# Folding and transform of the next sequence in pieces between chunks, with activation and sums placed after the block-end copies

## Chip, cores and metric

One Trainium2 chip, one of its cores. The metric is the device time of one execution of the whole kernel in microseconds, median of three runs.

## What is computed

Eight sequences of 3008 rows by 256 features go through a two-dimensional Fourier transform of which the real part is kept; each row of the result then goes through a two-layer block with a squared relu between the layers.

```python
batch, seq, dim = (8, 3008, 256)          # x
X = np.fft.fft(x, axis=1)
X = np.fft.fft(X, axis=2)
x = X.real.reshape(B * S, D)
h = x @ w_in                              # 256 x 2048
r = np.maximum(h, 0.0)
return (r * r) @ w_out                    # 2048 x 256
```

All in float32. A matmul of float32 appears in the profile as two records (two passes), and two weight loads.

## The kernel before

**Setting up.** The weights w_in are rounded on DVE (`rounded`, lines 137 to 154, nine DVE instructions for a load of 512 KB), and TensorE folds the transform over the features into them (`G1`, `G2`, `gE`). The tables of the transform over the rows stay in SBUF. w_out is rounded in the same way, a piece of it at the head of each of the first eight steps (`load_wout`).

**A sequence in two stages.** First the transform over the rows. `fold` (lines 191 to 212) takes one of the six row tiles of a sequence and adds and subtracts it with itself: eight DVE instructions with both inputs in SBUF, one small ScalarE copy of edge columns (line 204), and, on SP's queue, the load of the row tile that comes four later (`load_x`). It leaves `wP` and `wQ`. Then six groups of `dft_ops` (lines 214 to 259) multiply them with the tables: `even_n` is three matmuls into a PSUM tile `pd` and a ScalarE copy to `da`; `odd_n` is three matmuls into a second `pd` and two DVE instructions that write `Pt`, `Qt` or `Et`, a sequence's transform. The pool of `pd` has two buffers, and the transposes `po` of `store` use the same two.

**Then 48 steps**: six blocks of 251 or 250 columns by eight values of j. A step has these parts:

- `front` (lines 262 to 282): two chunks (the loop over h). Each is two matmuls into a PSUM tile `ph` (two buffers, so one for each chunk) and three DVE instructions (lines 275, 277, 278) that write half of the tile `g`. Then ScalarE applies relu and square to all of `g` in place.
- `combine` (lines 286 to 295): four GpSimd instructions form the sums `s` of `g`, on the left side of a Strassen-like product.
- `back` (lines 299 to 312): seven matmuls of `g` and `s` with w_out, accumulated over the eight j in four PSUM tiles mA to mD. `back` runs two steps behind `front` (LAG = 2).
- At a block's end `gather` (lines 314 to 333): ScalarE copies mA and mB to SBUF (`sA`, `sB`), DVE forms three sums `u`, GpSimd four sums `c`. Two steps later `store` transposes `c` on TensorE into `po`, copies it on ScalarE and sends it out on SP's queue.

**What sets the order.** The scheduling is manual: every engine runs its instructions in the order in which the program issues them. The main loop (lines 359 to 382) issues, for step i: `front(i)`, `combine(i)`, then the work for the next sequence, then `store` if one is due, then `back(i-2)` and, at a block's end, `gather`. The next sequence's folds stand whole behind the fronts of steps 1, 2, 4, 5, 7 and 8 of a sequence; its transform stands in rows of five operations at steps 10 and 18 and three at step 26. The last sequence has no such work, as none comes after it.

Of the kernel before, what the change touches and what calls it, by code (L numbers as in the profile page):

```python
# [42 lines left out]
def kernel(  # L43
# [12 lines left out]
    nc = tc.nc  # L56
    B, NROW, _, D = x.shape
# [5 lines left out]
    H = D // 2  # L63
    NJ = NFC // 2
    CH = 256
    CK = 251
    NT = 6
    NX = 4
# [7 lines left out]
    fp = ctx.enter_context(tc.tile_pool(name="fp", bufs=2))  # L76
    wp = ctx.enter_context(tc.tile_pool(name="wp", bufs=NT))
# [5 lines left out]
    op = ctx.enter_context(tc.tile_pool(name="op", bufs=2))  # L83
# [106 lines left out]

    def fold(b, t):

        rows = TILES[t][1]
        r = slice(0, rows)
        v = xt[b, t]
        s = fp.tile([P, 2, D], F32, name="fs", tag="fs")
        d = fp.tile([P, 2, D], F32, name="fd", tag="fd")
        tt(out=s[r], in0=v[r, 0::2], in1=v[r, 1::2], op=ALU.add)
        tt(out=d[r], in0=v[r, 0::2], in1=v[r, 1::2], op=ALU.subtract)
        if b * NT + t + NX < B * NT:  # L200
            load_x(*divmod(b * NT + t + NX, NT))
        sc = fp.tile([P, 2, H + 1], F32, name="sc", tag="sc")
        dc = fp.tile([P, 2, H - 1], F32, name="dc", tag="dc")
        nc.scalar.copy(sc[r, :, 0:H + 1:H], s[r, :, 0:H + 1:H])
        tt(out=sc[r, :, 1:H], in0=s[r, :, 1:H], in1=s[r, :, D - 1:H:-1], op=ALU.add)
        tt(out=dc[r], in0=d[r, :, 1:H], in1=d[r, :, D - 1:H:-1], op=ALU.subtract)
        wP = wp.tile([P, 2, H + 1], F32, name="wP", tag="wP")
        wQ = wp.tile([P, 2, H - 1], F32, name="wQ", tag="wQ")
        for kp in range(2):
            tt(out=wP[r, kp], in0=sc[r, 0], in1=sc[r, 1], op=ALU.subtract if kp else ALU.add)  # L210
            tt(out=wQ[r, kp], in0=dc[r, 0], in1=dc[r, 1], op=ALU.add if kp else ALU.subtract)  # L211
        folded[b, t] = (wP, wQ)

    def dft_ops(b):

        ops = []

        def start():
            PQE[b] = [pq.tile([n, NKT], F32, name=nm, tag=nm)
                      for nm, n in (("Pt", P), ("Qt", P - 1), ("Et", P))]  # L220

        def group(kp, which, st):
            nk = NK[kp]
            n = P - 1 if which == 1 else P
            tab = sinT if which == 1 else cosT

            def product(half):
                ps = psd.tile([P, 512], F32, name="pd", tag="d")[0:n, 0:nk]
                for i in range(3):
                    t = 3 * half + i  # L230
                    rows = TILES[t][1]
                    w = folded[b, t][which % 2][0:rows, kp]
                    w = w[:, H:H + 1].to_broadcast([rows, n]) if which == 2 else w[:, 0:n]
                    nc.tensor.matmul(ps, w, tab[0:rows, kp, t, 0:nk],  # L234
                                     start=i == 0, stop=i == 2)
                return ps

            def even_n():
                ps = product(0)
                st["a"] = hp.tile([P, NK[0]], F32, name="da", tag="da", bufs=2)[0:n, 0:nk]  # L240
                nc.scalar.copy(st["a"], ps)  # L241
# [12 lines left out]
            return [even_n, odd_n]  # L254

        for kp in range(2):
            for which in range(3):
                ops += group(kp, which, {})
        return [start] + ops


    def front(b, k0, n, j):

        pt, qt, et = PQE[b]
        ks = slice(k0, k0 + n)
        g = gp.tile([P, 2, 2, CK], F32, name="g", tag="g")
        for h in range(2):
            fc = j + NJ * h
            fs = slice(fc * P, (fc + 1) * P)
            ps = psh.tile([P, 2, CH], F32, name="ph", tag="h")  # L270
            hP, hQ = ps[:, 0, 0:n], ps[:, 1, 0:n]
            nc.tensor.matmul(hP, G1[:, fs], pt[:, ks], start=True, stop=True)  # L272
            nc.tensor.matmul(hQ, G2[:, fs], qt[:, ks], start=True, stop=True)  # L273
            t = hp.tile([P, CK], F32, name="he", tag="he")[:, 0:n]
            nc.vector.scalar_tensor_tensor(out=t, in0=et[:, ks], scalar=gE[:, fc:fc + 1], in1=hP,  # L275
                                           op0=ALU.mult, op1=ALU.add)
            tt(out=g[:, h, 0, 0:n], in0=t, in1=hQ, op=ALU.add)  # L277
            tt(out=g[:, h, 1, 0:n][:, ::-1], in0=t, in1=hQ, op=ALU.subtract)  # L278
        v = g[:, :, :, 0:n]
        act(v, v, AF.Relu)  # L280
        act(v, v, AF.Square)  # L281
        return g

    def combine(n, g):
# [4 lines left out]
        gt(out=s1, in0=g21, in1=g22, op=ALU.add)  # L291
# [7 lines left out]
    def back(n, j, g, s):  # L299

        if j == 0:
            for nm in ("mA", "mB", "mC", "mD"):
                acc[nm] = psm.tile([P, 2, CH], F32, name=nm, tag=nm)
        for nm, i, w, v in (("mA", 0, wout[:, 0, j, 0:H], g[:, 0, 0]),
                            ("mA", 1, wout[:, 1, j, 0:H], g[:, 1, 0]),
                            ("mB", 0, wsum[:, 2, j], g[:, 1, 1]),
                            ("mB", 1, wout[:, 0, j, H:D], s[:, 0]),
                            ("mC", 0, wsum[:, 0, j], s[:, 1]),
                            ("mC", 1, wsum[:, 1, j], s[:, 2]),
                            ("mD", 0, wout[:, 1, j, H:D], s[:, 3])):  # L310
            nc.tensor.matmul(acc[nm][:, i, 0:n], w, v[:, 0:n], start=j == 0 and i == 0, stop=j == NJ - 1,  # L311
                             skip_group_check=True)
# [38 lines left out]
    for f in [lambda t=t: fold(0, t) for t in range(NT)] + dft_ops(0):  # L351
# [6 lines left out]
    dft = []  # L358
    for i in range(len(steps) + LAG + 3):
        at = i % per  # L360
        if i < len(steps):
            b, k0, n, j = steps[i]
            if i < NJ:
                load_wout(i)
            g = front(b, k0, n, j)
            flight.append((b, k0, n, j, g, combine(n, g)))
            if b + 1 < B:
                if at < 9 and at % 3:
                    fold(b + 1, at // 3 * 2 + at % 3 - 1)
                if at == 10:  # L370
                    dft = dft_ops(b + 1)
        if at >= 10 and at % NJ == 2:
            for f in dft[:5]:
                f()
            dft = dft[5:]
        while finished and finished[0][0] <= i:
            store(*finished.pop(0)[1:])
        if i >= LAG and flight:
            b, k0, n, j, g, s = flight.pop(0)
            back(n, j, g, s)  # L380
            if j == NJ - 1:
                finished.append((i + 2, b, k0, n, gather(n)))


# [61 lines left out]
```

## Time and profile before

| | |
|---|---|
| median of three runs | 2365.93 us (2365.11 to 2368.36) |
| the profiled execution: its own time | 2366.93 us |
| the profiled execution: span of its instructions | 2365.2 us |
| mean granted TensorE clock | 0.959 |
| PE, busy (9504 matmul records) | 2138.7 us, 90% |
| DVE, busy | 1310.8 us, 55% |
| POOL, busy | 1168.7 us, 49% |
| ACT, busy | 920.7 us, 39% |

PE is the matmul side of TensorE and PEld its weight loads; DVE is VectorE, ACT ScalarE, POOL GpSimd, SP the queue of transfers. A row of the profile's groups or of the timeline names line, engine, operation and tiles (out<-in); a bracket gives the idle time of the engine ahead of it, and who ended it. A window's row gives the busy time of each engine with its number of instructions, and PEclk, the share of TensorE's full clock that was granted.

### The profile page before, as it was taken

Reading aid. Unit: us, or ns where it says so; the run is one execution under the profiler, and the core shown is the slowest. Engines: PE = TensorE matmul, PEld = TensorE weight load, DVE = VectorE, ACT = ScalarE, POOL = GpSimd, SP = SyncE. Lnnn points to the kernel's source line nnn. Section 1 sums busy time; section 2 is a strip of 40 time slices with the busy share of each in tenths; the row PEclk is TensorE's granted clock in tenths of the full one; section 3 lists DMA queues with packets and bytes.
Section 4 is the critical chain, followed back from the end, with each engine's and each line's share of the span. In section 5 each row is a group of like instructions: output and inputs, shape, how many; then the busy total and the mean of one; then the engine's idle time right before and its main releaser. Section 6 shows DMA issues by size and latency. Waiting matters only on the chain.

```text
span 2365.2 us, 26858 instructions
## 1 busy us (share of the span) xinstructions
PE 2138.7 (90%) x9504; PEld 1788.6 (76%) x9504; DVE 1310.8 (55%) x3076; ACT 920.7 (39%) x1065; POOL 1168.7 (49%) x1776
## 2 busy tenths in 40 slices
PE   3656999989998899979999799988999889999998
PEld 2334788767887788867888688876888777888887
DVE  5587445664457545584456744566445844455553
ACT  0012344433443344434344334443344333444453
POOL 0044356544565445544456445654456545556655
PEclk7778999999999999999999899999999999999999
DMA  5211000110001000020000100011000000000000
GB/s 189 70 62 44 9 18 10 42 37 10 10 18 44 27 9 18 10 61 9 10 18 27 44 10 18 10 44 36 9 10 18 27 10 9 18 10 18 10 18 18
DMA packets 38371, 64.31 MB, mean 27 GB/s; under 512 B 3285, under 2 KB 27605, under 8 KB 37725
## 3 DMA queue, kind: packets, MB, share of 16 engines
q1 hardware_dynamic: 35981, 54.63, 7.7%
q0 software_dynamic: 1440, 7.72, 0.9%
q8 instruction: 74, 1.21, 0.2%
q14 instruction: 60, 0.49, 0.1%
q10 hardware_dynamic: 816, 0.26, 0.0%
HBM read 37.96 MB, written 24.64 MB: 26 GB/s over the span
## 4 chain that ended last, share of the span: by engine, by line
PE 71%; DVE 17%; ACT 7%; POOL 2%; issue 1%; DMA 1%; ACTq 0%; DVEq 0%; SPq 0%; POOLq 0%
PE ph L272 12%; PE ph L273 11%; PE mA L311 11%; PE mB L311 11%; PE mC L311 11%; PE mD L311 6%; PE pd L234 5%; ACT g L280 3%; ACT g L281 3%; DVE g L277 2%; DVE he L275 2%; DVE g L278 2%; PE po L345 2%; DVE wP L210 2%; DVE wQ L211 1%
## 5 line engine op out<-in xcount | busy, mean ns | idle before, releaser
L280 ACT ACTIVATE g<-g 128x1004 f32<-128x1004 f32 (+1 forms) x384 | 399.2, 1040 | 1246.2 <-DVE g L278 845.7
L291 POOL TENSOR_TENSOR s<-g 128x251 f32<-128x251 f32 (+1 forms) x384 | 243.0, 633 | 1001.1 <-ACT g L281 913.7
L275 DVE SCALAR_TENSOR_TENSOR he<-Et,gE,ph 128x251 f32<-128x251 f32 (+1 forms) x768 | 362.5, 472 | 656.3 <-PE ph L273 656.0
L272 PE MATMUL ph<-Pt,G 128*128 128x251 f32 (+1 forms) x1536 | 472.5, 389 | 106.2 <-DVE g L278 104.9
L273 PE MATMUL ph<-Qt,G 127*128 127x251 f32 (+1 forms) x1536 | 466.1, 385 | 0.0
L272 PEld LDWEIGHTS ph<-Pt,G 128*128 128x128 f32 x1536 | 291.0, 194 | 170.5 <-DVE g L278 136.0
L311 PE MATMUL mC<-s,wsum 128*128 128x251 f32 (+1 forms) x1536 | 392.7, 377 | 14.8 <-DVE u L326 14.8
L281 ACT ACTIVATE g<-g 128x1004 f32<-128x1004 f32 (+1 forms) x384 | 399.1, 1039 | 12.1
L311 PE MATMUL mA<-g,wout 128*128 128x251 f32 (+1 forms) x1536 | 393.5, 378 | 0.0
L277 DVE TENSOR_TENSOR g<-he,ph 128x251 f32<-128x251 f32 (+1 forms) x768 | 320.5, 417 | 57.3 <-POOL s L293 0.5
L311 PEld LDWEIGHTS mC<-s,wsum 128*128 128x128 f32 x1536 | 292.4, 191 | 52.6 <-issue 17.0
L273 PEld LDWEIGHTS ph<-Qt,G 127*128 127x128 f32 x1536 | 300.7, 196 | 39.4
L311 PEld LDWEIGHTS mA<-g,wout 128*128 128x128 f32 x1536 | 288.6, 192 | 44.0 <-ACT sA L321 4.1
L278 DVE TENSOR_TENSOR g<-he,ph 128x251 f32<-128x251 f32 (+1 forms) x768 | 314.1, 409 | 0.0
L292 POOL TENSOR_TENSOR s<-s,g 128x251 f32<-128x251 f32 (+1 forms) x384 | 281.0, 732 | 30.1
L293 POOL TENSOR_TENSOR s<-g 128x251 f32<-128x251 f32 (+1 forms) x384 | 287.9, 750 | 0.0
L294 POOL TENSOR_TENSOR s<-g,s 128x251 f32<-128x251 f32 (+1 forms) x384 | 247.1, 644 | 0.0
L311 PE MATMUL mD<-s,wout 128*128 128x251 f32 (+1 forms) x768 | 226.4, 376 | 0.0
L311 PE MATMUL mB<-g,wsum 128*128 128x251 f32 (+1 forms) x768 | 226.0, 375 | 0.0
L311 PE MATMUL mB<-s,wout 128*128 128x251 f32 (+1 forms) x768 | 224.6, 374 | 0.0
L234 PE MATMUL pd<-cosT,wP 128*128 128x377 f32 (+5 forms) x384 | 140.9, 513 | 27.0 <-ACT da L241 15.1
L311 PEld LDWEIGHTS mB<-g,wsum 128*128 128x128 f32 x768 | 146.6, 191 | 18.2
(63 smaller groups left out, 1382.0 us busy)
## 6 DMA issues: line engine op xcount, KB each, us to landing
xt<-in_x_dram SPq DMA_DIRECT2D x28, 512.0 KB
out_dram<-os SPq DMA_DIRECT2D x96, 125.0 KB
out_dram<-os SPq DMA_DIRECT2D x80, 126.0 KB
raw<-in_moe_w_in_dram SPq DMA_DIRECT2D x8, 512.0 KB
raw<-in_moe_w_out_dram SPq DMA_DIRECT2D x8, 512.0 KB
xt<-in_x_dram SPq DMA_DIRECT2D x7, 484.0 KB
xt<-in_x_dram SPq DMA_DIRECT2D x7, 480.0 KB
cosT<-in_cos_s_dram POOLq DMA_DIRECT2D x2, 1131.0 KB, 18.0
```

What stands on the lines that cost most here:

```text
L234: nc.tensor.matmul(ps, w, tab[0:rows, kp, t, 0:nk], start=i == 0, stop=i == 2)
L272: nc.tensor.matmul(hP, G1[:, fs], pt[:, ks], start=True, stop=True)
L273: nc.tensor.matmul(hQ, G2[:, fs], qt[:, ks], start=True, stop=True)
L275: nc.vector.scalar_tensor_tensor(out=t, in0=et[:, ks], scalar=gE[:, fc:fc + 1], in1=hP, op0=ALU.mult, op1=ALU.add)
L277: tt(out=g[:, h, 0, 0:n], in0=t, in1=hQ, op=ALU.add)
L278: tt(out=g[:, h, 1, 0:n][:, ::-1], in0=t, in1=hQ, op=ALU.subtract)
L280: act(v, v, AF.Relu)
L281: act(v, v, AF.Square)
L292: gt(out=s2, in0=s1, in1=g11, op=ALU.subtract)
L293: gt(out=s3, in0=g11, in1=g21, op=ALU.subtract)
L294: gt(out=s4, in0=g12, in1=s2, op=ALU.subtract)
L311: nc.tensor.matmul(acc[nm][:, i, 0:n], w, v[:, 0:n], start=j == 0 and i == 0, stop=j == NJ - 1, skip_group_check=True)
```

## The change

`fold` no longer issues anything by itself: it returns six pieces, each with a nominal cost, and `dft_ops` returns its operations with such costs. `front` calls `between()` after each of its two chunks; `between` issues pieces from the list of the next sequence as the costs fall due, at an even pace over the sequence's 96 chunks less six (in the first sequence over 80 less six, since nothing is issued in its first eight steps). The edge copy goes from ScalarE to DVE. Relu and square move from `front` to `combine`, and `combine(i)` is issued at the end of step i: after the store, `back(i-2)` and the block-end copies and sums.

```diff
     def fold(b, t):
...
-        tt(out=s[r], in0=v[r, 0::2], in1=v[r, 1::2], op=ALU.add)
-        tt(out=d[r], in0=v[r, 0::2], in1=v[r, 1::2], op=ALU.subtract)
-        if b * NT + t + NX < B * NT:
-            load_x(*divmod(b * NT + t + NX, NT))
...
-        nc.scalar.copy(sc[r, :, 0:H + 1:H], s[r, :, 0:H + 1:H])
...
+        def f_s():
+            v = xt[b, t]
+            tt(out=new(fp, "fs", [P, 2, D])[r], in0=v[r, 0::2], in1=v[r, 1::2], op=ALU.add)
+
+        def f_d():
+            v = xt[b, t]
+            tt(out=new(fp, "fd", [P, 2, D])[r], in0=v[r, 0::2], in1=v[r, 1::2], op=ALU.subtract)
+            if b * NT + t + NX < B * NT:
+                load_x(*divmod(b * NT + t + NX, NT))
+
+        def f_sc():
+            s, sc = st["fs"], new(fp, "sc", [P, 2, H + 1])
+            nc.vector.tensor_copy(sc[r, :, 0:H + 1:H], s[r, :, 0:H + 1:H])
...
+        return [(0.7, f_s), (0.7, f_d), (0.5, f_sc), (0.4, f_dc), (0.6, f_p), (0.6, f_q)]
...
-            return [even_n, odd_n]
+            return [(0.6, even_n), (1.2, odd_n)]
...
-    def front(b, k0, n, j):
+    def front(b, k0, n, j, between):
...
             tt(out=g[:, h, 1, 0:n][:, ::-1], in0=t, in1=hQ, op=ALU.subtract)
+            between()
+        return g
...
+    def combine(n, g):
         v = g[:, :, :, 0:n]
         act(v, v, AF.Relu)
         act(v, v, AF.Square)
-        return g
...
+    def ahead(b):
+        return [piece for t in range(NT) for piece in fold(b, t)] + dft_ops(b)
...
+    side, spent, pace = [], 0.0, 0.0
+
+    def between():
+
+        nonlocal spent
+        if i < NJ:
+            return
+        spent -= pace
+        while side and spent <= 0:
+            t, f = side.pop(0)
+            f()
+            spent += t
...
     for i in range(len(steps) + LAG + 3):
-        at = i % per
         if i < len(steps):
             b, k0, n, j = steps[i]
             if i < NJ:
                 load_wout(i)
-            g = front(b, k0, n, j)
-            flight.append((b, k0, n, j, g, combine(n, g)))
-            if b + 1 < B:
-                if at < 9 and at % 3:
-                    fold(b + 1, at // 3 * 2 + at % 3 - 1)
-                if at == 10:
-                    dft = dft_ops(b + 1)
-        if at >= 10 and at % NJ == 2:
-            for f in dft[:5]:
-                f()
-            dft = dft[5:]
+            if i % per == 0:
+                assert not side
+                side = ahead(b + 1) if b + 1 < B else []
+                spent, pace = 0.0, sum(t for t, _ in side) / (2 * (per - (0 if i else NJ)) - 6)
+            g = front(b, k0, n, j, between)
         while finished and finished[0][0] <= i:
             store(*finished.pop(0)[1:])
         if i >= LAG and flight:
...
+            at, g_, s_ = flight.pop(0)
+            back(at[2], at[3], g_, s_)
+            if at[3] == NJ - 1:
+                finished.append((i + 2, *at[:3], gather(at[2])))
+        if i < len(steps):
+            flight.append(((b, k0, n, j), g, combine(n, g)))
```

On DVE, in step 2 of the second sequence before the change, a whole fold stands between two fronts (`he` and `g` are a chunk's three instructions, `fs` to `wQ` the fold's tiles):

```order
L278 TENSOR_TENSOR g<-he,ph 128x251
L198 TENSOR_TENSOR fs<-xt 128x512
L199 TENSOR_TENSOR fd<-xt 128x512
L205 TENSOR_TENSOR sc<-fs 128x2x127
L206 TENSOR_TENSOR dc<-fd 128x254
L210 TENSOR_TENSOR wP<-sc 128x129
L211 TENSOR_TENSOR wQ<-dc 128x127
L210 TENSOR_TENSOR wP<-sc 128x129
L211 TENSOR_TENSOR wQ<-dc 128x127
L275 SCALAR_TENSOR_TENSOR he<-Et,gE,ph 128x251
```

On DVE after the change, in steps 3 and 4 of the second sequence, there is one piece of that fold between two chunks (the same three instructions for a chunk, now lines 295, 297 and 298):

```order
L298 TENSOR_TENSOR g<-he,ph 128x251
L224 TENSOR_TENSOR wP<-sc 128x129 x2
L295 SCALAR_TENSOR_TENSOR he<-Et,gE,ph 128x251
L297 TENSOR_TENSOR g<-he,ph 128x251
L298 TENSOR_TENSOR g<-he,ph 128x251
L295 SCALAR_TENSOR_TENSOR he<-Et,gE,ph 128x251
L297 TENSOR_TENSOR g<-he,ph 128x251
L298 TENSOR_TENSOR g<-he,ph 128x251
L229 TENSOR_TENSOR wQ<-dc 128x127 x2
L295 SCALAR_TENSOR_TENSOR he<-Et,gE,ph 128x251
```

The eight fold instructions in a row have become pieces of one or two, with three or six of the front's instructions between them.

On PE before the change, at step 10 of a sequence, the products of two groups of the transform stand in one row behind the front (`ph`) and ahead of the back (`mA` and so on):

```order
L272 MATMUL ph<-Pt,G_104 128x251
L273 MATMUL ph<-Qt,G_105 128x251
L234 MATMUL pd<-cosT,wP 128x377 x6
L234 MATMUL pd<-sinT,wQ 127x377 x6
L311 MATMUL mA<-g,wout 128x251 x2
```

On PE after the change, at step 35 of the second sequence, one product of three matmuls stands behind the front, here with a store's transposes (`po`) right behind it:

```order
L293 MATMUL ph<-Qt,G_105 128x251
L254 MATMUL pd<-cosT,wP 128x377 x3
L366 MATMUL po<-ident,c 126x128 x8
L332 MATMUL mA<-g,wout 128x251 x2
L332 MATMUL mB<-g,wsum 128x251
```

Twelve products that stood in three rows are spread over steps 29 to 43, one to a step at most, and this one has come to stand ahead of a store.

On ACT before the change, at a block's end, the copies `sA` and `sB` stand behind the relu and square of the step in which they are issued, and the copies `da` of the transform follow two at a time:

```order
L280 ACTIVATE g<-g 128x1004
L281 ACTIVATE g<-g 128x1004
L321 COPY sA<-mA 128x502
L322 COPY sB<-mB 128x502
L280 ACTIVATE g<-g 128x1004
L281 ACTIVATE g<-g 128x1004
L241 COPY da<-pd 128x377
L241 COPY da<-pd 127x377
```

On ACT after the change, at the same block's end (lines 306 and 307 are relu and square):

```order
L307 ACTIVATE g<-g 128x1004
L342 COPY sA<-mA 128x502
L343 COPY sB<-mB 128x502
L306 ACTIVATE g<-g 128x1004
L307 ACTIVATE g<-g 128x1004
L306 ACTIVATE g<-g 128x1004
```

The two copies now come ahead of that step's relu and square, and no `da` copy follows them here.

More of the change, by code (lines that the diff above doesn't have):

```diff
@@ L194, in fold @@
         r = slice(0, rows)
[L195 to L198, printed above, removed]
-        tt(out=d[r], in0=v[r, 0::2], in1=v[r, 1::2], op=ALU.subtract)
-        if b * NT + t + NX < B * NT:
-            load_x(*divmod(b * NT + t + NX, NT))
-        sc = fp.tile([P, 2, H + 1], F32, name="sc", tag="sc")
-        dc = fp.tile([P, 2, H - 1], F32, name="dc", tag="dc")
@@ L204, in fold @@
-        nc.scalar.copy(sc[r, :, 0:H + 1:H], s[r, :, 0:H + 1:H])
[L205 to L211, printed above, removed]
@@ L212, in fold, with new @@
-        folded[b, t] = (wP, wQ)
+        st = {}
+        def new(pool, nm, shape):
+            st[nm] = pool.tile(shape, F32, name=nm, tag=nm)
+            return st[nm]
+        def f_s():
[6 more added lines that the diff above has]
+                load_x(*divmod(b * NT + t + NX, NT))
@@ new lines, in f_sc, with f_dc, f_p @@
+        def f_sc():
+            s, sc = st["fs"], new(fp, "sc", [P, 2, H + 1])
+            nc.vector.tensor_copy(sc[r, :, 0:H + 1:H], s[r, :, 0:H + 1:H])
+            tt(out=sc[r, :, 1:H], in0=s[r, :, 1:H], in1=s[r, :, D - 1:H:-1], op=ALU.add)
+        def f_dc():
+            d = st["fd"]
+            tt(out=new(fp, "dc", [P, 2, H - 1])[r], in0=d[r, :, 1:H], in1=d[r, :, D - 1:H:-1], op=ALU.subtract)
+        def f_p():
+            sc, wP = st["sc"], new(wp, "wP", [P, 2, H + 1])
+            for kp in range(2):
+                tt(out=wP[r, kp], in0=sc[r, 0], in1=sc[r, 1], op=ALU.subtract if kp else ALU.add)
@@ L214, in dft_ops, with f_q @@
+        def f_q():
+            dc, wQ = st["dc"], new(wp, "wQ", [P, 2, H - 1])
+            for kp in range(2):
+                tt(out=wQ[r, kp], in0=dc[r, 0], in1=dc[r, 1], op=ALU.add if kp else ALU.subtract)
+            folded[b, t] = (st["wP"], wQ)
+        return [(0.7, f_s), (0.7, f_d), (0.5, f_sc), (0.4, f_dc), (0.6, f_p), (0.6, f_q)]
     def dft_ops(b):
@@ L258, in dft_ops @@
                 ops += group(kp, which, {})
-        return [start] + ops
-    def front(b, k0, n, j):
+        return [(0.0, start)] + ops
+    def front(b, k0, n, j, between):
         pt, qt, et = PQE[b]
@@ L281, in front @@
         act(v, v, AF.Square)
-        return g
-    def combine(n, g):
         s = sp.tile([P, 4, CK], F32, name="s", tag="s")
@@ L349, in store @@
                 nc.sync.dma_start(out=out[row + c0:row + c1], in_=os_[c0 - o:c1 - o, i])
-    for f in [lambda t=t: fold(0, t) for t in range(NT)] + dft_ops(0):
+    def ahead(b):
+        return [piece for t in range(NT) for piece in fold(b, t)] + dft_ops(b)
+    for _, f in ahead(0):
         f()
@@ L356 @@
     per = len(BLOCKS) * NJ
+    side, spent, pace = [], 0.0, 0.0
[8 more added lines that the diff above has]
+            spent += t
     flight, finished = [], []
-    dft = []
     for i in range(len(steps) + LAG + 3):
-        at = i % per
         if i < len(steps):
@@ L378 @@
         if i >= LAG and flight:
[L379 to L382, printed above, removed]
+            at, g_, s_ = flight.pop(0)
[4 more added lines that the diff above has]
+            flight.append(((b, k0, n, j), g, combine(n, g)))
 _INS = ['x', 'moe_w_in', 'moe_w_out', 'cos_s', 'sin_s', 'cos_d', 'sin_d', 'alt_d']
```

## Prediction

> **What bounds the kernel now.** I read the page first, then the windows by stage, the waits of PE, and the timeline where PE stood still.
>
> ```profile
> PE 2138.7 (90%) x9504; PEld 1788.6 (76%) x9504; DVE 1310.8 (55%) x3076; ACT 920.7 (39%) x1065; POOL 1168.7 (49%) x1776
> 0.00:115.05 115.05, 59.23 (x167) 31.97 (x168) 61.41 (x134) 9.89 (x21) 6.19 (x16) 0.76 0.39 133
> 115.05:206.10 91.05, 45.43 (x150) 35.43 (x148) 81.45 (x152) 14.93 (x18) 35.79 (x59) 0.76 0.18 58
> 206.10:436.85 230.75, 221.36 (x991) 186.24 (x992) 115.45 (x286) 96.12 (x109) 118.34 (x182) 0.98 0.06 16
> 436.85:2117.10 1680.25, 1575.28 (x7058) 1324.59 (x7057) 932.25 (x2196) 685.11 (x793) 862.79 (x1296) 0.98 0.07 22
> 2117.10:2342.40 225.30, 225.30 (x1083) 199.82 (x1082) 116.71 (x300) 109.07 (x119) 137.78 (x212) 1.00 0.05 15
> 2342.40:2365.20 22.80, 12.13 (x60) 10.51 (x59) 3.50 (x9) 5.63 (x8) 7.80 (x12) 0.84 0.07 22
> ```
>
> The windows (length, then busy time of PE, PEld, DVE, ACT and POOL, then PEclk) are: set-up to the first step; steps 0 to 7 of the first sequence; its other 40 steps; sequences 2 to 7; 47 steps of the last sequence; its last step and the drain. In the last sequence PE is busy all 225.30 us at clock 1.00: without folds and transform nothing but PE limits a step. In sequences 2 to 7 it is not: 1680.25 us for six, 280.0 each, PE idle for 105 of them and the clock at 0.98. In the first eight steps DVE is the busy one, 81.45 of 91.05 us.
>
> The number of steps and the price of one come from line 272 (four records a step) and the timeline of the last sequence:
>
> ```profile
> 2117.10:2342.40 225.30, 55.22 (x188) 35.36 (x188) 1.00 0.05 15
> 2256.72 0.58 PE L272 MATMUL ph<-Pt,G 128*128 128x251 f32 x2
> 2257.77 0.48 DVE L275 SCALAR_TENSOR_TENSOR he<-Et,gE,ph 128x251 f32<-128x251 f32 x1 [2.19 <-PE ph L273]
> 2257.86 0.63 POOL L291 TENSOR_TENSOR s<-g 128x251 f32<-128x251 f32 x1 [3.02 <-ACT g L281]
> 2258.69 0.41 DVE L278 TENSOR_TENSOR g<-he,ph 128x251 f32<-128x251 f32 x1
> 2259.85 0.41 DVE L278 TENSOR_TENSOR g<-he,ph 128x251 f32<-128x251 f32 x1
> 2261.40 0.58 PE L272 MATMUL ph<-Pt,G 128*128 128x251 f32 x2
> 2261.44 1.04 ACT L281 ACTIVATE g<-g 128x1004 f32<-128x1004 f32 x1
> 2262.56 0.63 POOL L291 TENSOR_TENSOR s<-g 128x251 f32<-128x251 f32 x1 [2.00 <-ACT g L281]
> ```
>
> 188 records are 47 steps. One step is 2261.40 - 2256.72 = 4.68 us. 47 of them are 220.0; the other 5.3 us are the six stores, 0.89 each. A clean sequence is 225.30 + 4.68 = 230.0 us. The same rows give the slack. DVE is idle 2.19 us in a step. A chunk's bank of `ph` is free 2.38 us after the step's start (2259.10) and wanted again at 4.68; the second's at 3.54 and about 5.53. The sums begin 5.84 us after the step's start (2262.56 - 2256.72), and the first of them is done at 6.47; `back` two steps later wants it at 2 x 4.68 + 7 matmuls of 4.68/11 = 12.3: 5.9 us of slack.
>
> Where PE stood still:
>
> ```profile
> PE ph L272 <- DVE g L278: 104.9, 38, 8.4
> PE pd L234 <- ACT da L241: 35.4, 14, 3.9
> 100.16 7.78 PE L234 MATMUL pd<-cosT,wP 128*128 128x377 f32 x24
> 107.77 3.96 PE L234 MATMUL pd<-sinT,wQ 128*127 128x376 f32 x12
> 1063.39 0.69 PE L272 MATMUL ph<-Pt,G 128*128 128x251 f32 x2 [2.97 <-DVE g L278]
> 1066.39 4.51 PE L234 MATMUL pd<-cosT,wP 128*128 128x377 f32 x12
> 1073.43 5.76 PE L234 MATMUL pd<-sinT,wQ 128*127 128x377 f32 x12 [2.53 <-ACT da L241]
> ```
>
> PE waits for DVE to free a bank of `ph` (the folds stand in front of the next front), and in the transform's rows for the copies `da`. Waits of 2.5 to 3 us bring a slow clock behind them: twelve passes took 5.76 us at 1073.43, and at 100.16 twenty-four took 7.61 to the next start, 0.317 each. A sequence's 72 passes of the transform are thus 22.8 us when nothing waits, and a sequence with all its work is 230.0 + 22.8 = 252.8 us on PE, against 280.0.
>
> **The change part by part.**
>
> *Sequences 2 to 7.* The number of matmuls stays. If pieces fit into DVE's slack, PE runs through: 1680.25 - 6 x 252.8 = 163.4 us less. Do they fit? A fold in place:
>
> ```profile
> 1005.98 0.96 DVE L198 TENSOR_TENSOR fs<-xt 128x512 f32<-128x512 f32 x1
> 1010.05 0.81 DVE L210 TENSOR_TENSOR wP<-sc 128x129 f32<-128x129 f32 x1
> 1011.42 0.80 DVE L210 TENSOR_TENSOR wP<-sc 128x129 f32<-128x129 f32 x1
> 1012.14 0.28 DVE L211 TENSOR_TENSOR wQ<-dc 128x127 f32<-128x127 f32 x1
> 22.87 0.16 DVE L174 COPY gE<-pe 128x4 f32<-128x4 f32 x1 [7.53 <-PE pe L172]
> ```
>
> From 1005.98 to 1012.42 it took 6.44 us, a wait for the edge copy among them. Six are 38.6 us, 0.8 us a step; the largest piece is the two of `wP`, 1.6 us. Each is under the slack of 2.0 to 2.3 us of a bank. The worst step by the order (step 9: `wQ`, `fs`, and the block end's three `u`, 1.2 us) asks 1.5 + 1.0 + 1.2 = 3.7 us of DVE where 2.19 are idle; the 1.5 left over go into the next step, still inside the banks' slack. What was hidden by nothing before (a whole fold) is now hidden by PE's own 4.68 us. The odd products' two DVE additions wait for PE's three matmuls (1.9 us) while PE does the rest of the step; that step is 1.9 us longer on PE, so DVE has the time for it. The edge copy on DVE is nearest to the copy of 0.16 us at 22.87; ScalarE's copy and the wait for it go. On SP, the loads of `x` stand behind a piece that DVE has done in the same step, so stores behind them wait no longer than that.
>
> *One new wait.* At step 35 an odd product stands right ahead of a store whose second transpose tile takes that product's buffer. PE does four transposes (0.45 us, half the 0.89) while DVE's two additions end about 1.3 us after the product: I put a stall of 0.9 us there, once in each of seven sequences, 6.3 us. What a short stall does to the clock is the open price:
>
> ```profile
> 1015.97 0.30 PEld L272 LDWEIGHTS ph<-Pt,G 128*128 128x128 f32 x2 [0.44 <-DVE g L278]
> 1015.97 0.69 PE L272 MATMUL ph<-Pt,G 128*128 128x251 f32 x2
> 1023.02 1.16 PE L272 MATMUL ph<-Pt,G 128*128 128x251 f32 x2 [2.08 <-DVE g L278]
> ```
>
> The two records at 1015.97 came after a wait of 0.44 us and took 0.69; those at 1023.02 came after 2.08 us and took 1.16, where a clean step has 0.58. By the second row, and the slow stretch at 1073.43 (5.76 us for what 12 x 0.317 = 3.8 should do), a stall could cost 2.0 us more, 20 us in all seven; by the first it costs its own length, 6.3. A stall of 0.9 lies nearer to the first, and I take 6.3. The Trainium skill (TensorE: Matmul & The Clock Gate, "What's actually happening") has the clock fall only after an idle window of about 3.4 us; by that rule the sum would be 6.3, but the slow pair after 2.08 us speaks against that length as a limit, so the larger figure stays in the range.
>
> *Block ends.* The copies `sA` and `sB` now precede relu and square of that step, and GpSimd's `c` precede the sums `s`. `sA` waits for the second of the back's matmuls, `sB` for the fourth; they stand some 1 us ahead of the relu's due time. On POOL the four `c` (2.7 us) delay `s` by less than 3 us of the slack of 5.9. Cost nothing; if the slack were gone, each us of delay would be a us of PE.
>
> *First sequence, steps 0 to 7.* No pieces there: the five folds that DVE did among the roundings go to later steps.
>
> ```profile
> 121.66 0.47 DVE L275 SCALAR_TENSOR_TENSOR he<-Et,gE,ph 128x251 f32<-128x251 f32 x1
> 130.86 0.47 DVE L275 SCALAR_TENSOR_TENSOR he<-Et,gE,ph 128x251 f32<-128x251 f32 x1
> 134.88 0.43 SPq L128 DMA_DIRECT2D raw<-in_moe_w_out_dram  x1
> 139.66 0.43 DVE L137 TENSOR_SCALAR fs<-raw 128x512 uint32<-128x512 uint32 x1 [0.64 <-DMA raw<-in_moe_w_out_dram]
> 153.96 0.43 DVE L137 TENSOR_SCALAR fs<-raw 128x512 uint32<-128x512 uint32 x1 [1.03 <-DMA raw<-in_moe_w_out_dram]
> 161.39 0.42 DVE L137 TENSOR_SCALAR fs<-raw 128x512 uint32<-128x512 uint32 x1
> ```
>
> A step without a fold took 9.2 us beside POOL's sums (121.66 to 130.86) and 7.43 without them (153.96 to 161.39). I take 9.2, since the sums now always run beside the rounding: 8 x 9.2 = 73.6, less 1.3 for the first: 72.3 against 91.05, 18.8 us less. Below, 8 x 7.43 = 59.4, another 12.9 less. A load of w_out now follows the last read of the buffer before by 4.8 us (134.88 to 139.66), which that step just covers.
>
> *Its other 40 steps:* 40 x 4.68 + 5 stores x 0.89 + 22.8 = 214.5 against 230.75, 16.3 us less. The set-up gains six edge copies on DVE, 1.0 us. The last sequence stays.
>
> *Sum:* 2366.9 (the profiled execution, 1.7 over its span) - 163.4 - 16.3 - 18.8 + 1.0 + 6.3 = 2175.7. That execution lies 1.0 above the median of the runs, 2365.93, so the median should be about **2175 us**.
>
> **The rivals.** *Pieces that PE feels:* fold instructions have both inputs in SBUF, and beside POOL's sums `wP` took 0.81 us, at other times 0.28 (its neighbour at 1012.14). If POOL and DVE hold each other up and this reached PE with one POOL sum (0.72 us, four fill 2.7) for each of 36 fold pieces in seven sequences, 181 us would come back: 2356; a tenth of them, 2193. Against it: the slack of 5.9 us at the sums and of 2 us at the banks. The Trainium skill (SBUF — State Buffer, "Who interferes with whom") makes such a pair of instructions exclude each other for a whole instruction; by that rule the cause is there, and the 0.81 against 0.28 agrees, but it says nothing of the slack.
>
> *The clock does not hold:* PE would be near 100% busy for 2000 us, the trace shows full clock for 225. If it fell to the mean 0.96 of before, 4% of 2000 us: 2255. Nothing in the trace shows a fall while PE is busy.
>
> *Slower, by the block ends:* on ACT, relu waits behind `sA`, which waits for a back, which waits for sums two steps older, which waited for a relu. If that loop runs late by more than 5.9 us, PE stalls at `mB` at each of 48 block ends. From 191/48 = 4.0 us a block end beyond the slack, 9.9 us of delay, all is lost; at 5 us it is 2415. The delays that I count add to 3.
>
> *The pieces do not spread:* the order excludes it, they stand between chunks.
>
> **How the numbers follow.** Forecast 0.86; pieces that PE feels 0.08; the clock 0.03; slower by the block ends 0.03. Low end: 2175 less 12.9 (roundings unhindered), less a third of the 6.3: 2160. High end: 2175 + 14 (slow clock behind the seven stalls) + near a tenth of the fold pieces felt (18): 2205 or so. A measurement here can tell 0.2% (4.7 us) from no change; faster 0.96, same 0.01, slower 0.03.
>
> **What would show it.** Right: the windows of sequences 2 to 7 at 253 to 255 us with PE busy throughout and PEclk 1.00; PE's waits for `g` and `da` nearly gone; steps 0 to 7 near 72 us. Wrong: PE waits for `s` (block ends) or for `g` with many short entries; PEclk under 1 with PE busy; PE waiting at `po` behind `pd` for more than 0.9 us.

## The result, and the profile after

The change takes the kernel from 2365.52 to **2173.93 us** (median of four runs, 2173.75 to 2174.41), a ratio of 0.9188 with a 95% interval of 0.9172 to 0.9204. The profiled execution took 2173.86 us over a span of 2172.1. The forecast was 2175, and its terms can be checked one by one in the windows of the changed kernel, cut at the same stages as before (length; busy PE, PEld, DVE, ACT, POOL; PEclk):

```profile
0.00:115.55 115.55, 58.48 (x168) 31.71 (x169) 62.50 (x140) 8.80 (x15) 6.18 (x16) 0.76 0.38 133
115.55:188.00 72.45, 44.45 (x151) 34.13 (x149) 69.33 (x120) 14.57 (x14) 38.62 (x59) 0.81 0.14 44
188.00:403.40 215.40, 214.68 (x992) 183.91 (x993) 135.13 (x324) 97.03 (x107) 124.44 (x182) 1.00 0.09 27
403.40:1924.20 1520.80, 1516.75 (x7058) 1309.71 (x7057) 930.40 (x2232) 690.97 (x757) 877.67 (x1296) 1.00 0.08 24
1924.20:2149.15 224.95, 224.95 (x1084) 200.56 (x1083) 117.20 (x300) 110.45 (x119) 137.88 (x212) 1.00 0.05 15
2149.15:2172.10 22.95, 12.69 (x60) 10.98 (x58) 3.50 (x9) 5.68 (x8) 7.80 (x12) 0.80 0.07 22
```

From the first sequence's ninth step to the last step PE is busy in all but 4.8 us, and its clock stands at 1.00 throughout. DVE does as much as before (930 against 932 us in sequences 2 to 7); it does it in the time that PE needs anyway.

What PE still waits for, in the whole kernel (sum, times, longest):

```profile
PE pg L167 <- DVE win L154: 47.4, 4, 15.4
PE ph L292 <- DVE g L298: 27.9, 8, 5.7
PE pd L254 <- DVE wP L224: 7.0, 5, 2.0
PE po L366 <- ACT os L368: 4.7, 7, 0.7
```

The first and third stand in the set-up, the second in the first eight steps, where DVE rounds w_out. Only the last is in the steady part: seven times 0.7 us, once in each of seven sequences. It is the stall that was forecast, a store behind an odd product. In sequences 2 to 7 it stands at step 35, as forecast; in the first sequence, whose pieces are paced over fewer chunks, it stands at step 43. PE and DVE show it in the timeline of the third sequence, step 35:

```profile
1088.90 2.07 PE L254 MATMUL pd<-cosT,wP 128*128 128x377 f32 x6
1090.80 0.60 PE L366 MATMUL po<-ident,c 128*126 128x128 f32 x4
1091.07 0.55 DVE L267 TENSOR_TENSOR Et<-da,pd 128x377 f32<-128x377 f32 x1 [0.34 <-PE pd L254]
1091.54 0.54 DVE L272 TENSOR_TENSOR Et<-da,pd 128x376 f32<-128x376 f32 x1
1092.08 0.66 PE L366 MATMUL po<-ident,c 128*126 128x128 f32 x4 [0.68 <-ACT os L368]
```

The second four transposes start at 1092.08, when DVE's second addition ends (1091.54 + 0.54). The bracket names ScalarE's copy, which ended at about the same time: a wait for several is put down to one of them. The odd product and the store together took 8.35 us with their step where 4.68 + 1.90 + 0.89 = 7.47 were due, 0.88 more.

### The profile page after: what moved, and what is told of

Same layout as the page of the kernel before. It is cut to its first block, busy times and chain, and to the rows that moved or that the text cites. A ratio compares the mean times of both kernels' runs of the same rounds, so it can differ in the third digit from the quotient of the medians.

```text
span 2172.1 us, 26892 instructions
## 1 busy us (share of the span) xinstructions
PE 2072.0 (95%) x9504; PEld 1771.0 (82%) x9504; DVE 1318.1 (61%) x3124; ACT 927.5 (43%) x1017; POOL 1192.6 (55%) x1776
## 4 chain that ended last, share of the span: by engine, by line
PE 93%; DVE 6%; issue 0%; ACT 0%; DMA 0%; POOL 0%; POOLq 0%; DVEq 0%
PE mC L332 15%; PE mA L332 15%; PE mB L332 15%; PE ph L293 15%; PE ph L292 15%; PE pd L254 8%; PE mD L332 7%; PE po L366 2%; PE pg L167 1%; DVE fs L153 1%; DVE fs L145 1%; DVE fs L139 1%; DVE fd L144 1%; DVE fs L151 0%; DVE fd L149 0%; DVE fd L143 0%
## 5 line engine op out<-in xcount | busy, mean ns | idle before, releaser
L292 PE MATMUL ph<-Pt,G 128*128 128x251 f32 (+1 forms) x1536 | 455.6, 378 | 28.0 <-DVE g L298 27.9
L293 PE MATMUL ph<-Qt,G 127*128 127x251 f32 (+1 forms) x1536 | 455.4, 377 | 0.0
L293 PEld LDWEIGHTS ph<-Qt,G 127*128 127x128 f32 x1536 | 293.8, 191 | 36.9
L315 POOL TENSOR_TENSOR s<-g,s 128x251 f32<-128x251 f32 (+1 forms) x384 | 259.8, 676 | 0.0
L332 PE MATMUL mD<-s,wout 128*128 128x251 f32 (+1 forms) x768 | 225.0, 374 | 0.0
L332 PEld LDWEIGHTS mD<-s,wout 128*128 128x128 f32 x768 | 144.9, 189 | 18.1
```

## The experiments

Each was compared with the kernel before in the same session; the medians of the kernel before were 2365.5 to 2367.6 us there.

### What the size of a piece is worth: whole folds, spread evenly

```diff
-        return [(0.7, f_s), (0.7, f_d), (0.5, f_sc), (0.4, f_dc), (0.6, f_p), (0.6, f_q)]
+        def whole():
+            for f in (f_s, f_d, f_sc, f_dc, f_p, f_q):
+                f()
+        return [(3.5, whole)]
```

> The changed kernel, but each fold is one piece again (all eight additions in a row), still spread evenly, one fold to four or five steps; the transform stays in pieces. Theory (a piece must fit into the slack of about 2 us that a bank of ph has): a lump of some 5.8 us behind the first chunk of a step stalls PE by 5.8 - 2.0 = 3.8 us, behind the second chunk by about 1.8 us; 12 of the one and 30 of the other give 46 + 54 = 100 us, and slow clock behind the longer stalls up to 20 more: 2260 to 2295 us. Rival (spreading is enough, since back runs two steps behind and evens a lump out): 2174 to 2185 us.

Measured: 2209.5 us (2207.9 to 2211.2), 36 more than the changed kernel. Both expectations missed: the lump costs, but a third of what I worked out. About 15 of the 36 us lie in the first sequence and 20 in the six after it. In those one fold of six, the one behind the first chunk of the sequence's first step, makes PE's next step 2.2 us longer, or 3.9 in one of them; the others cost about 1 us together. The timeline of DVE in this kernel shows what I had too large, in the second sequence:

```profile
443.20 0.69 DVE L204 TENSOR_TENSOR fs<-xt 128x512 f32<-128x512 f32 x1
444.40 0.17 DVE L214 COPY sc<-fs 128x4 f32<-128x4 f32 x1
444.94 0.42 DVE L219 TENSOR_TENSOR dc<-fd 128x254 f32<-128x254 f32 x1
446.53 0.47 DVE L299 SCALAR_TENSOR_TENSOR he<-Et,gE,ph 128x251 f32<-128x251 f32 x1
```

This fold took 3.33 us (443.20 to 446.53), not 5.8; the 42 folds in the steps of this run took 3.3 to 4.8 us, 3.9 in the mean. The one that makes PE wait took 4.0 us, and 4.0 less the slack of 2.0 is near the 2.2 measured: the rule for the price held, the length in it did not. Before the change a fold took 5.8 to 6.9 us. In the one that the prediction shows (6.44 us) this is what stretched it (DVE, then ScalarE, of the kernel before):

```profile
1006.86 0.68 DVE L199 TENSOR_TENSOR fd<-xt 128x512 f32<-128x512 f32 x1
1008.41 0.87 DVE L205 TENSOR_TENSOR sc<-fs 128x254 f32<-128x254 f32 x1 [0.87 <-ACT sc L204]
1009.20 0.93 DVE L206 TENSOR_TENSOR dc<-fd 128x254 f32<-128x254 f32 x1
```

```profile
1006.17 1.04 ACT L280 ACTIVATE g<-g 128x1004 f32<-128x1004 f32 x1 [2.55 <-DVE g L278]
1007.25 1.04 ACT L281 ACTIVATE g<-g 128x1004 f32<-128x1004 f32 x1
1008.19 0.18 ACT L204 COPY sc<-fs 128x4 f32<-128x4 f32 x1
```

The edge copy of 0.18 us stood behind a relu and a square of 2 us. DVE waited 0.87 us for it, and by the time it went on, GpSimd's sums had begun (at 1008.37): `dc` took 0.93 us beside them and 0.42 without. Every fold in the steps before the change waited so, for 0.2 to 1.2 us. The wait is not the only way to meet the sums, as the run with the order alone shows below. The Trainium skill (SBUF — State Buffer, "Who interferes with whom") says that a VectorE instruction with two inputs in SBUF and a GpSimd one that reads SBUF hold each other up; the 0.93 against 0.42 agrees.

### The order of the block end: undone, and alone

The change has two main parts, so each was run without the other (the edge copy's move to DVE stays with the pieces). First the pieces with the old order:

```diff
             g = front(b, k0, n, j, between)
+            flight.append(((b, k0, n, j), g, combine(n, g)))
...
-        if i < len(steps):
-            flight.append(((b, k0, n, j), g, combine(n, g)))
```

> The changed kernel with the order of the block end undone: relu, square and the sums of a step are issued right behind its front again, ahead of the store, the back and the block-end copies; the pieces stay. Theory (the pieces are all of the gain, the order is hidden by the slack of 5.9 us at the sums): 2172 to 2182 us; the waits of mA for the copy sA, 0.2 us at a block end, come back, at most 0.2 x 48 = 10 us. Rival (the order carries a part of the gain): 2190 us or more.

Measured: 2194.5 us (2193.2 to 2195.1), ratio 0.9278 (0.9264 to 0.9291): 20.5 us slower than with both. The order carries a part of the gain, as the rival had it. A sequence loses 2.8 us, nearly all of it next to block ends: 0.9 us at step 10, 0.4 at step 11 and 1.1 at step 19. At step 10 of the third sequence `sA` stands behind a square, and PE waits for it:

```profile
712.30 1.04 ACT L307 ACTIVATE g<-g 128x1004 f32<-128x1004 f32 x1
713.25 0.56 ACT L342 COPY sA<-mA 128x502 f32<-128x502 f32 x1
713.86 1.11 PE L332 MATMUL mA<-g,wout 128*128 128x251 f32 x4 [0.61 <-ACT sA L342]
```

Ahead of step 19 DVE's sums `u` wait 2.1 us for the next such copy, and PE then waits 0.8 us for a bank of `ph`. Then the old folds and rows with the new order (relu and square stand at the head of `combine`):

```diff
             g = front(b, k0, n, j)
-            flight.append((b, k0, n, j, g, combine(n, g)))
...
             if j == NJ - 1:
                 finished.append((i + 2, b, k0, n, gather(n)))
+        if i < len(steps):
+            flight.append((b, k0, n, j, g, combine(n, g)))
```

> The kernel before with only the order changed: relu, square and sums behind the block-end copies; folds whole and transform in rows as before. Theory: the waits for sA go (4.1 us in all), nothing else: 2358 to 2368 us. Rival (the order carries a part of the gain): below 2350 us. Rival (relu behind the copies runs late): above 2375 us.

Measured: **2227.5 us** (2226.6 to 2230.0), ratio 0.9420 (0.9406 to 0.9434): 138 us faster than before, where I had expected 4. My theory that the pieces are all of the gain falls. What the pieces alone take off is 171 us, what the order alone takes off 138, and both together 192: they do much of the same work. One of sequences 2 to 7 takes 280.0 us before, 259.1 with the order, 256.3 with the pieces, 253.5 with both; PE needs 252.5. Of the order's 138 us about half (71) comes from steps 2 to 9, where the folds stand, and half (68) from steps 10, 18 and 26 with the transform. In steps 0 to 7 of the first sequence it gives nothing (91.9 us from the first front to that of step 8, against 90.8 before); the 18.7 us there come from the pieces, which go elsewhere.

How the order works by itself is plain at step 10, where the transform stands in a row. ScalarE before the change:

```profile
1070.91 1.04 ACT L280 ACTIVATE g<-g 128x1004 f32<-128x1004 f32 x1 [3.23 <-DVE g L278]
1071.98 1.04 ACT L281 ACTIVATE g<-g 128x1004 f32<-128x1004 f32 x1
1072.92 0.46 ACT L241 COPY da<-pd 128x377 f32<-128x377 f32 x1
```

ScalarE and PE with the order alone:

```profile
739.32 0.47 ACT L241 COPY da<-pd 128x377 f32<-128x377 f32 x1 [0.91 <-PE pd L234]
743.13 0.47 ACT L241 COPY da<-pd 127x377 f32<-127x377 f32 x1 [3.33 <-PE pd L234]
743.50 1.04 ACT L285 ACTIVATE g<-g 128x1004 f32<-128x1004 f32 x1
```

```profile
737.22 3.97 PE L234 MATMUL pd<-cosT,wP 128*128 128x377 f32 x12
741.03 3.97 PE L234 MATMUL pd<-sinT,wQ 128*127 128x377 f32 x12
```

Before, the copy `da` stood behind a relu that waited 3.23 us for DVE, and PE waited 2.53 us for a free buffer of `pd`. With relu behind it, the copy waits for nothing but its product, and PE runs both rows without a gap: 3.97 us each, where the second took 5.76.

For the folds the order does less. None waits for its edge copy any more, but in most sequences three of the six still take 5.6 to 6.0 us, since GpSimd's sums run beside them. One of them (DVE, GpSimd and ScalarE with the order alone):

```profile
696.12 0.69 DVE L198 TENSOR_TENSOR fs<-xt 128x512 f32<-128x512 f32 x1
696.18 1.21 POOL L292 TENSOR_TENSOR s<-s,g 128x251 f32<-128x251 f32 x1
696.84 0.20 ACT L204 COPY sc<-fs 128x4 f32<-128x4 f32 x1 [3.55 <-DVE fs L198]
701.77 0.46 DVE L275 SCALAR_TENSOR_TENSOR he<-Et,gE,ph 128x251 f32<-128x251 f32 x1
```

From 696.12 to 701.77 it took 5.65 us with no wait for ScalarE in it.

### Which part of the order: relu only behind the next sequence's work

```diff
             dft = dft[5:]
+        if i < len(steps):
+            flight.append((b, k0, n, j, g, combine(n, g)))
         while finished and finished[0][0] <= i:
```

This is the order alone with `combine` one place further up: behind fold and transform, ahead of store, back and block-end copies.

> The kernel before with relu, square and sums of a step moved only a part of the way: behind the next sequence's fold and transform, but still ahead of the store, the back and the block-end copies. Theory (what the order gains by itself, 138 us, comes from ScalarE's small copies for the fold and the transform no longer standing behind a relu and a square that wait for DVE): 2222 to 2245 us, nearly all of it. Rival (it comes from the block-end copies and the store's copies standing ahead of relu, as the change puts it): 2340 to 2366 us.

Measured: 2231.3 us (2230.7 to 2231.9), 136 below the kernel before in its session (2367.6), where the whole order took off 138. So with whole folds and rows it is the place of relu, square and sums behind the folds and the transform that matters, where the edge copies and the `da` copies no longer stand behind relu. What the later sums on GpSimd give of this was not run apart. The block-end copies, by which the change is named, are worth a few us at most in this kernel, as its 4.1 us of waits for `sA` say too:

```profile
PE ph L272 <- DVE g L278: 58.5, 20, 8.4
PE mA L311 <- ACT sA L321: 4.1, 6, 0.7
PE pd L234 <- ACT da L241: 3.9, 7, 0.6
```

With the pieces in, it is the other way round: the 20 us of the run with the old order lie next to the block ends.

### The transform in rows again

```diff
-        return [piece for t in range(NT) for piece in fold(b, t)] + dft_ops(b)
+        return [piece for t in range(NT) for piece in fold(b, t)]
...
             g = front(b, k0, n, j, between)
+            if b + 1 < B and i % per == 34:
+                dft = dft_ops(b + 1)
+            if i % per in (34, 38, 42):
+                for _, f in dft[:5]:
+                    f()
+                dft = dft[5:]
```

> The changed kernel, but the transform of the next sequence stands in rows of five, five and three operations again (at steps 34, 38 and 42 of a sequence); the folds stay in pieces. Theory (products in a row make PE wait for the copies da and the additions): what steps 10, 18 and 26 lost before, 46.2 - 3 x 4.68 - 22.8 = 9.3 us a sequence, comes back in seven sequences: 2174 + 65 = 2239 us, 2225 to 2250. Rival (the folds in the way of the front were all of it): 2174 to 2180 us.

The pace of the folds stays as it was. Measured: 2167.5 us (2166.7 to 2168.3), 6 us *faster* than the changed kernel and below the rival's range too. The theory is wrong as put: rows do not make PE wait once `da` is ahead of relu. The two windows are steps 34 and 38 of the third sequence:

```profile
818.85:831.15 12.30, 12.30 (x47) 8.70 (x46) 5.52 (x13) 4.62 (x6) 6.39 (x11) 1.00 0.01 1
846.05:860.25 14.20, 14.20 (x54) 9.83 (x53) 4.36 (x10) 4.67 (x7) 2.61 (x4) 1.00 0.01 1
```

PE is busy in all of both; 12.30 us is 4.68 + 4 x 1.90. The 6 us are the seven stalls at the store, since no row meets one.

### Even pace or small pieces: two pieces to a step

```diff
+                side = [(1.0 if t else 0.0, f) for t, f in side]
-                spent, pace = 0.0, sum(t for t, _ in side) / (2 * (per - (0 if i else NJ)) - 6)
+                spent, pace = 1.0, 1.0
```

> The changed kernel with one piece behind every chunk until the list is empty, so two to a step: all folds in 18 steps, the transform in the next 6, nothing after. Theory (the size of a piece decides, not the even pace): DVE has 2.45 us of front and 1.8 us of pieces in a step of 4.68, and only block ends ask for more: 2174 to 2200 us. Rival (the even pace is needed): DVE is full in these steps and each runs over by 1 us or more, 18 steps in 7 sequences, with the transform's rows on top: 2290 us or more.

Measured: 2174.4 us (2173.9 to 2174.8), the same as the changed kernel. The 18 steps with the folds of the third sequence, in one window:

```profile
657.50:743.40 85.90, 85.90 (x413) 76.57 (x412) 67.94 (x168) 42.51 (x47) 59.17 (x80) 1.00 0.17 49
```

DVE is 79% busy there, PE without a gap. The even pace is not needed; one small piece behind each chunk is enough.

### How much DVE has to spare: twelve more instructions to a sequence

```diff
             tt(out=new(fp, "fs", [P, 2, D])[r], in0=v[r, 0::2], in1=v[r, 1::2], op=ALU.add)
+            tt(out=st["fs"][r], in0=v[r, 0::2], in1=v[r, 1::2], op=ALU.add)
```

and the same for `fd`: both instructions are issued twice.

> The changed kernel with the first addition and the first subtraction of each fold issued twice, so 12 instructions of some 0.8 us more for DVE in a sequence, 9.6 us of DVE in each of seven sequences (and 9.6 in the set-up, where they add some 8 us, since PE waits for them there; the result is the same). Theory (pieces lie in DVE's idle time, 2.19 us a step): 2174 + 8 = 2182 us, at most 2190. Rival (PE feels each fold instruction): 67 us more, 2250 us.

Measured: 2184.1 us (2184.0 to 2184.1), 10 more. The set-up ends 9.1 us later (115.55 to 124.65), and a sequence in the loop takes what it took:

```profile
0.00:124.65 124.65, 59.39 (x168) 31.96 (x169) 70.75 (x152) 8.80 (x15) 6.38 (x16) 0.74 0.35 123
412.80:666.30 253.50, 252.82 (x1177) 218.16 (x1176) 164.41 (x384) 115.01 (x127) 149.00 (x216) 1.00 0.08 25
```

Some 9 us more of DVE in a sequence cost nothing (164.41 us busy, 155.01 in the changed kernel). What costs is the set-up, where no matmuls cover it.

### The edge copy back on ScalarE

```diff
-            nc.vector.tensor_copy(sc[r, :, 0:H + 1:H], s[r, :, 0:H + 1:H])
+            nc.scalar.copy(sc[r, :, 0:H + 1:H], s[r, :, 0:H + 1:H])
```

> The changed kernel with the edge copy of each fold back on ScalarE. Theory (DVE waits 0.9 us for the copy, but inside its idle time): 2170 to 2178 us; the set-up may even gain 1 us. Rival (the copy on ScalarE stands behind relu and square, DVE waits 2 us and more and frees the banks late): each of 36 copies in the loop of seven sequences costs PE 0.5 us or more: 2190 us or more.

Measured: 2176.2 us (2173.7 to 2176.5), within the theory; sequences of 253.5 us as in the changed kernel. The engine of the copy does not matter here, where it no longer stands behind a waiting relu. In the old order the copy was not moved by itself.

### The slack at the sums: back one step behind front

```diff
-    LAG = 2
+    LAG = 1
```

> The changed kernel with back one step behind front instead of two, so that the slack at the sums falls by a step, from 5.9 to 1.2 us at the first and about 0.4 at the last of the four. Theory (the lag of two hides the later relu and sums at a block end): at 48 block ends the sums stand behind the four c on GpSimd, 1.7 us or more later, and PE stalls 1 to 2 us: 50 to 100 us more, and pieces behind the first chunk of a step delay relu by 0.8 to 1.9 us and stall PE by up to 1 us at some 120 places, 30 to 80 more: 2250 to 2350 us. Rival (the delays of relu and sums are nothing that the lag has to hide): 2174 to 2185 us.

> As the run with a lag of one, but with relu, square and sums right behind the front again. Theory (the new order costs the sums 1.7 us or more at a block end, which only the lag of two hides): 40 to 90 us less than the run with the new order. Rival (the order is the same with little slack): within 10 us of that run.

Measured: 2267.0 us (2266.0 to 2268.1) with the new order, 93 more than with the lag of two, and 2246.7 (2245.7 to 2247.7) with the old one. The lag does hide later sums, as the theory has it, but the difference of the orders is 20 us, neither the 40 to 90 of the theory nor the rival's 10. Nor do the 93 us belong to the new order: with the old one the shorter lag costs 52. In 47 steps of the last sequence, where no pieces stand, PE takes 232.9 us with the new order, 228.3 with the old and 225.0 with a lag of two. The waits of PE with the new order, then with the old:

```profile
PE mA L332 <- ACT g L307: 11.2, 25, 1.1
PE mB L332 <- POOL s L312: 8.3, 25, 0.9
```

```profile
PE mA L332 <- ACT g L307: 11.4, 32, 1.1
PE mA L332 <- ACT sA L342: 7.3, 13, 0.9
```

Both wait for relu and square, and both for the sums at `mC` and `mD` (15.7 us with the new order, 8.6 with the old). Where the new order waits for the sums at `mB` too, the old one waits at `mA` for the copies `sA` that stand behind relu. By steps, some 60 of the 93 us lie one step behind the block-end copies (steps 1, 9, 17, 25, 33 and 41), 1.3 us at each in the last sequence, and 24 at steps 4, 14 and 24, nearly all in sequences with pieces; the old order loses as much at these three. So both terms of the theory are there. The listed waits add to less, 35 us for these tiles with the new order. Each order has its own late party at a block's end, so undoing one brings out the other.

### The last stall, and the set-up

```diff
-                spent, pace = 0.0, sum(t for t, _ in side) / (2 * (per - (0 if i else NJ)) - 6)
+                spent, pace = 0.0, sum(t for t, _ in side) / (2 * (per - (0 if i else NJ)) - 8)
```

> The changed kernel with the pace set so that no odd product stands in a step with a store (the six chunks left over become eight). Theory (the stall of 0.88 us in a step where a store's transposes wait for the buffer of an odd product, once in each of seven sequences, is the only loss left in the steady part): 2174 - 6 = 2168 us, 2166 to 2170. Rival (the stall is of the store itself or moves to the next user of the buffers): 2173 to 2176 us.

Measured: 2167.2 us (2167.2 to 2167.3), ratio 0.9163 (0.9148 to 0.9178), 6.7 less than the changed kernel. A sequence is now PE's own time:

```profile
655.05:907.50 252.45, 252.45 (x1177) 218.46 (x1176) 152.66 (x372) 115.28 (x127) 146.95 (x216) 1.00 0.09 25
```

What is left lies ahead of the ninth step. In the set-up DVE waited four times for PE, 30.5 us in all, before a copy of 0.16 us (`gE`) that stood in its queue ahead of the next rounding:

```diff
-        nc.vector.tensor_copy(gE[:, c * WC // P:(c + 1) * WC // P], ps[:, 0:WC // P])
+        nc.scalar.copy(gE[:, c * WC // P:(c + 1) * WC // P], ps[:, 0:WC // P])
```

> The kernel without the meeting of odd product and store, and the four copies of gE in the set-up moved from DVE to ScalarE. Before, DVE stood still for them for 7 us at each of four chunks of w_in (30.5 us waiting for PE). Theory (the set-up of 115 us is now the largest part in which PE is not the bound, and DVE's wait is on its path): the rounding runs through and the set-up ends 20 to 28 us earlier: 2140 to 2150 us. Rival (the loads of x and of the tables are not there earlier): 2160 to 2168 us.

Measured: **2138.8 us** (2138.6 to 2140.7), ratio 0.9038 (0.9023 to 0.9053), the fastest of all and just under the expected range. The set-up, then the first eight steps:

```profile
0.00:87.30 87.30, 55.33 (x168) 30.91 (x169) 62.12 (x136) 9.45 (x19) 6.52 (x16) 0.86 0.50 175
87.30:159.70 72.40, 44.34 (x151) 33.81 (x149) 69.28 (x120) 14.57 (x14) 38.54 (x59) 0.81 0.14 44
```

The set-up is 28 us shorter, and DVE is busy for as long as before (62 us). It is the fault of the `da` copies turned round: there a small copy that could run stood behind an instruction that waits, here a small copy that waits stood ahead of work that could run.

## Why the prediction was right, and where its reasons were not

**The sum.** *Sequences 2 to 7:* 1680.25 to 1520.80, 159.5 us less, where 163.4 less six of the stalls (5.4) were forecast, 158.0. *The other 40 steps of the first sequence:* 230.75 to 215.40, 15.4 less; forecast 16.3 less one stall of 0.9. *Steps 0 to 7:* 72.45 us; forecast 72.3, and the step without sums beside it (7.43) did not come. *Set-up:* 0.5 us more, forecast 1.0. *The new stall:* 0.88 us, forecast 0.9, once in each of seven sequences, at step 35 in six of them and at step 43 in the first; the run that parts product and store gives 6.7 us, forecast 6.3. *The clock:* the stalls of 0.68 us left it at 1.00, so the lower price was the right one. The Trainium skill (TensorE: Matmul & The Clock Gate, "What's actually happening") lets the clock fall only after an idle window of about 3.4 us. The 0.68 us agree with that, but shorter idle times than 3.4 us were followed by a fall: right after PE's wait of 2.08 us before the change the granted clock was 0.50 for 3.4 us (from 1023.10), and with whole folds the same began 0.9 us after a wait of 1.93 us (at 240.53). *DVE's slack:* shown by the doubled instructions, some 9 us of DVE a sequence at no cost.

The sum was safe because it took the floor from a stage in which nothing but PE limits (the last sequence) and added the transform's matmuls at their own price. In sequences 2 to 7, whatever removes the waits ends at that floor.

**The step that failed** is "Block ends. [...] Cost nothing", in which the order of relu was weighed only for what it might cost. It was worth 138 us by itself, and 136 come without the block-end copies that the step weighs: relu, square and sums only have to go behind the folds and the transform, so that the edge copies and `da` copies no longer stand behind relu in ScalarE's queue. With the pieces in it was worth 20 us, and these do lie at the block ends, where `sA` stood behind relu. The row that told it was in the prediction (PE waits for `pd` because of `da`, 35.4 us) and was put down to products that stand in a row; the run with rows and the new order shows rows without any wait. In the same way "the folds stand in front of the next front" was true, but not why a fold was long: 5.8 to 6.9 us before, since it waited for ScalarE and ran beside GpSimd's sums, and 3.3 to 4.8 whole in the changed kernel. Neither changed the sum, as both parts were made together and end at the same floor: the total came out right by that, and not by the prices of the parts. As an account of which part does what the prediction was wrong, and so were the expectations of the runs with the order alone and the whole folds.

**The rivals.** Fold pieces that PE feels: no, sequences are 1.0 us over PE's time, and nearly all of that is the store's stall. A clock that does not hold: 1.00 over 1960 us of work. Slower by the block ends: the delays stayed inside the slack; with one step of slack taken away the new order is 20 us slower than the old one, so the mechanism is there, and the lag of two pays for it. That the loss would exceed the gain was not seen at any setting.

**Left open.** The 2.8 us a sequence that the old order costs with pieces lie next to block ends, but how they divide between `sA`, the store and DVE's sums was not run apart. With whole folds and rows, the edge copies, the `da` copies and the later sums were not moved one by one. And whole folds cost 15 us in the first sequence alone, where a step became up to 4.4 us longer; two of its waits (2.42 and 1.93 us) have 3.4 us at a granted clock of 0.50 behind them, others of 1.2 to 2.0 us have not.

## What to carry to other kernels

Take the floor from a stretch of the same trace in which the bound engine has nothing to wait for; what a set of fixes can give is the distance to that floor, and fixes that remove the same wait in two ways do not add up (171 and 138 us gave 192). In an engine's queue, look for a small copy that another engine needs behind a large instruction that waits, and for a small instruction that waits ahead of work that is ready: moving the first, with the sums behind it, gave this kernel about 136 us, moving the second 28. Before splitting work in pieces, ask what the long piece was waiting for, and what runs beside it.

## What the runs showed of the hardware

A fold on VectorE took 3.33 us when nearly all of it ran clear of GpSimd's sums and 6.44 when, after a wait of 0.87 us, its second half ran beside them: an addition of 0.42 us took 0.93 there. With no wait but the sums beside it a fold took 5.65 us. PE held the full clock for about 1960 us of nearly unbroken float32 matmuls, and gaps of 0.68 us left it there. Waits of 1.93 and 2.08 us were each followed by 3.4 us at a granted clock of 0.50; one of 1.91 us, with the order alone, was not.
